# A retention layer feeding two dense networks: decay masks by scans, two blocks of tokens sharing the accumulator banks of the first expert, and state products issued with the value products

## The chip, the core and the metric

The kernel runs on one core of a Trainium2 chip. The core has a matrix engine (TensorE, rows "PE", its weight loads "PEld"), three elementwise engines (VectorE "DVE", ScalarE "ACT", GpSimd "POOL") and a queue engine (SyncE "SP") that issues the transfers; 16 DMA engines carry these out. The metric is the time of one execution on the device, in microseconds (us), as the median of several runs.

## What is computed

Three stages follow each other: a block-wise retention (linear attention with a decay `lam` per head), a mixture of four experts with given gates, and one dense network.

```python
def _attn_ref(q, k, v, lam):            # B, H, S, D = 2, 8, 768, 64
    rel = pos[:, None] - pos[None, :]   # pos: places in a block
    Dmask = np.where(rel >= 0, lam[:, None, None] ** rel[None], 0.0)
    for b in range(nb):
        intra = einsum('bhic,bhjc->bhij', qb, kb) * Dmask[None]
        intra = einsum('bhij,bhjd->bhid', intra, vb)
        inter = einsum('bhid,bhde->bhie', qb * lam_pow[None], kv_state)
        out[:, :, sl] = intra + inter
        kv_state = lam_block * kv_state + einsum('bhsd,bhse->bhde', kb * rev_pow, vb)
...
def _moe_ref(x, domain_probs, w1, w2):  # 1536 tokens, width 512, 4 experts of 1024
    p = domain_probs / (domain_probs.sum(-1, keepdims=True) + 1e-09)
    for e in range(E):
        out += p[:, e:e + 1] * (np.maximum(x @ w1[e], 0.0) @ w2[e])
...
def _moe2_ref(x, w_in, w_out):          # inner width 2048
    h = x @ w_in
    return (h * (1.0 / (1.0 + np.exp(-h)))) @ w_out
```

## The kernel before

**Retention.** It works on blocks of 128 tokens, six per batch (c = 0 to 5), so twelve units u = 2c + b. A unit is cut into pieces. `prep` makes `qs` (queries times `qdec`, the powers of `lam`) and `old` (the decayed state), both on GpSimd. `scores` makes `ks` (decayed keys, GpSimd), multiplies keys by queries into two banks `s` on TensorE, and VectorE multiplies these by the mask `dmask` into `a`. `mix` forms the output `xps` from the state and from `a` and the values. `carry` forms the state products `sps` from `ks` and the values. These matmuls take plain float32.

**Masks.** `powers` writes the powers of `lam` into a small tile `z` by seven doublings on VectorE, stores it to device memory (`zd`) and loads it back with overlapping addresses: `dmask` then holds, for key place j and query place i, the power for i and j, and `qdec` the powers for a query place. Before and after the first scores, `keep_warm` gives TensorE matmuls on zeros ("warm").

**Experts.** Every operand of a matmul is kept as a high and a low part (`xhi`, `xlo`; weights `ua`, `ub` for up and `dh`, `dl` for down; hidden `hhi`, `hlo`), and three products are summed. ScalarE makes the high part, VectorE or GpSimd the low one (`split`, line 142). Phase "a" does the first 512 tokens (blocks c = 0 and 1 of both batches, 256 columns each), one expert after the other in eight steps f; a step has a `gemm1` (12 matmuls into `ph`) and, two steps later, a `gemm2` (12 matmuls into the four banks `po`). Weights come in pairs of steps: `("a", i)` serves f = 2i and 2i + 1, 512 KB up (`u`) and 512 KB down (`d`). For expert 0 the eight steps run once over columns 0 to 255 and once over columns 256 to 511, since block c = 1 is not ready earlier; each half has its own set of `po` banks, emptied by `evacuate`. Experts 1 to 3 run over 512 columns. In between come the pieces of units 2 to 11, spread over half-steps by `plan` and `attend`. Phase "a" has so 40 steps. The rest ("c" for the other 1024 tokens, "b" and "d" for the dense network) is the same in both kernels.

**Order.** All engines run their instructions in the order of the code, as `manual_schedule` says; transfers are issued by SP in that order as well, and a transfer into a buffer in use waits there for its readers, with all behind it.

## Time and profile before

| | |
|---|---|
| time, median of 3 runs | 816.2 us (815.89 to 816.4) |
| span of the profiled execution, first to last instruction | 814.1 us |
| TensorE busy | 807.5 us (99%) |
| VectorE, GpSimd, ScalarE busy | 529.7, 453.4, 326.4 us |
| first `gemm1` starts / step 16 (expert 1) starts | 15.67 / 77.30 us into the span |

Only the span is given of the profiled execution; its own time on the device is not listed. The span is 2.1 us under the median, for what lies around it. "Busy" of TensorE counts the warm matmuls and the switch from one kind of matmul to another, so 99% busy does not say that nothing can be taken out.

### The profile page before, as it was taken

What the parts mean: (1) busy time and instruction counts of PE and PEld (TensorE: products, weight loads), DVE (VectorE), ACT (ScalarE), POOL (GpSimd) and SP (SyncE); (2) the same over time, 40 slices, a digit from 0 to 9 for tenths busy, and PEclk for the clock granted to TensorE, in tenths of its full rate; (3) what the DMA queues carried; (4) which work ended last, traced back from release to release, by engine and by line L of the source; (5) the groups of instructions that cost most, each with busy time, mean ns of one, the idle gap of its engine ahead of it and who ended that gap; (6) DMA issues with size and microseconds to landing.
All of it is one profiled execution on the core that took longest, in us unless ns stands there. A gap on an engine that the chain in (4) does not pass through costs nothing.

```text
span 814.1 us, 11017 instructions
## 1 busy us (share of the span) xinstructions
PE 807.5 (99%) x4224; PEld 666.9 (82%) x4224; DVE 529.7 (65%) x762; ACT 326.4 (40%) x528; POOL 453.4 (56%) x333
## 2 busy tenths in 40 slices
PE   9999999999999999999999999999999999999998
PEld 5899877778888888888888888888888888888886
DVE  6375797545668588878888878865454345666666
ACT  3433332433446333333333333334454465444431
POOL 1824755525666666666666666754346666555631
PEclk9999999999999999999999999999999999999999
DMA  8885767533324223223322211122233131111002
GB/s 296 317 321 195 250 240 240 189 102 117 104 104 142 90 91 115 94 83 98 112 94 85 94 61 70 46 90 90 78 103 105 52 103 52 52 52 52 27 1 103
DMA packets 31434, 95.93 MB, mean 118 GB/s; under 512 B 3409, under 2 KB 5001, under 8 KB 31381
## 3 DMA queue, kind: packets, MB, share of 16 engines
q1 hardware_dynamic: 31380, 95.23, 35.1%
q8 instruction: 33, 0.54, 0.3%
q14 instruction: 21, 0.16, 0.1%
HBM read 83.65 MB, written 11.57 MB: 117 GB/s over the span
## 4 chain that ended last, share of the span: by engine, by line
PE 93%; DVE 3%; DMA 2%; issue 1%; ACT 1%; POOL 0%; SPq 0%; ACTq 0%; POOLq 0%
PE po L707 32%; PE po L525 14%; PE ph L470 14%; PE y L647 12%; PE x L647 8%; PE z L647 8%; PE warm L299 1%; PE s L374 1%; PE xps L401 1%; DMA words<-wts 1%; DMA u<-wts 1%; DVE dec L213 1%; DVE dec L209 1%; DVE tail L206 1%; PE xps L397 1%
## 5 line engine op out<-in xcount | busy, mean ns | idle before, releaser
L707 PE MATMUL po<-hlo,dh 128*128 128x512 f32 x384 | 149.6, 390 | 0.0
L707 PE MATMUL po<-hhi,dh 128*128 128x512 f32 x384 | 149.6, 390 | 0.0
L707 PE MATMUL po<-hhi,dl 128*128 128x512 f32 x384 | 149.6, 389 | 0.0
L719 DVE TENSOR_TENSOR acc<-po,acc 128x512 f32<-128x512 f32 x176 | 117.2, 683 | 43.2 <-PE po L707 43.2
L142 POOL TENSOR_TENSOR ub<-u,ua 128x256 fp32r<-128x256 f32 (+2 forms) x48 | 74.8, 1559 | 107.4 <-ACT ua L141 103.1
L142 POOL TENSOR_TENSOR dl<-d,dh 128x1024 fp32r<-128x1024 f32 (+1 forms) x48 | 114.3, 2380 | 28.8 <-ACT dh L141 28.8
L664 POOL TENSOR_TENSOR s<-s,s 128x512 f32<-128x512 f32 x48 | 63.2, 1319 | 50.3 <-ACT s L659 50.2
L142 POOL TENSOR_TENSOR uc<-u,uc 128x512 fp32r<-128x512 f32 x24 | 31.2, 1301 | 96.7 <-ACT uc L141 96.7
L707 PEld LDWEIGHTS po<-hhi,dl 128*128 128x128 f32 x384 | 72.1, 188 | 15.0
L707 PEld LDWEIGHTS po<-hhi,dh 128*128 128x128 f32 x384 | 72.1, 188 | 14.9
L707 PEld LDWEIGHTS po<-hlo,dh 128*128 128x128 f32 x384 | 72.1, 188 | 14.9
L497 ACT ACTIVATE hhi<-ph 128x512 fp32r<-128x512 f32 x40 | 23.9, 599 | 97.0 <-DVE ph L491 83.3
L142 POOL TENSOR_TENSOR ub<-us,ua 128x1024 fp32r<-128x1024 f32 x24 | 58.4, 2433 | 5.3 <-ACT ua L141 5.3
L525 PE MATMUL po<-hhi,dh 128*128 128x512 f32 (+1 forms) x224 | 58.7, 364 | 0.0
L525 PE MATMUL po<-hhi,dl 128*128 128x512 f32 (+1 forms) x224 | 57.7, 360 | 0.0
L525 PE MATMUL po<-hlo,dh 128*128 128x512 f32 (+1 forms) x224 | 57.6, 359 | 0.0
L470 PE MATMUL ph<-xhi,ua 128*128 128x512 f32 (+1 forms) x224 | 55.6, 371 | 1.2 <-DVE hlo L481 0.7
L141 ACT ACTIVATE dh<-d 128x1024 fp32r<-128x1024 f32 (+1 forms) x52 | 51.3, 988 | 9.2 <-POOL ub L142 2.6
L470 PE MATMUL ph<-xhi,ub 128*128 128x512 f32 (+1 forms) x224 | 53.1, 359 | 0.0
L470 PE MATMUL ph<-xlo,ua 128*128 128x512 f32 (+1 forms) x224 | 53.1, 359 | 0.0
L498 DVE TENSOR_TENSOR hlo<-ph,hhi 128x512 fp32r<-128x512 f32 x40 | 27.7, 692 | 27.8 <-ACT hhi L497 27.8
L470 PEld LDWEIGHTS ph<-xhi,ua 128*128 128x128 f32 x224 | 37.9, 189 | 9.4 <-DVE hlo L481 0.9
(128 smaller groups left out, 1577.7 us busy)
## 6 DMA issues: line engine op xcount, KB each, us to landing
u<-wts SPq DMA_DIRECT2D x32, 512.0 KB, 3.6
d<-wts SPq DMA_DIRECT2D x32, 512.0 KB, 3.7
words<-wts SPq DMA_DIRECT2D x32, 512.0 KB, 5.1
wd<-dec SPq DMA_DIRECT2D x32, 256.0 KB, 3.1
u<-wd SPq DMA_DIRECT2D x16, 512.0 KB, 3.7
d<-wd SPq DMA_DIRECT2D x16, 512.0 KB, 3.7
qkt<-qk SPq DMA_DIRECT2D x12, 512.0 KB, 5.9
kvt<-kv SPq DMA_DIRECT2D x10, 512.0 KB, 5.6
```

Source lines behind the costliest of these rows:

```text
L141: nc.scalar.activation(out=hi, in_=src, func=AF.Copy)
L142: eng.tensor_tensor(out=lo, in0=src, in1=hi.bitcast(F32), op=ALU.subtract)
L206: nc.vector.tensor_scalar(out=tail, in0=low, scalar1=2.0 ** -29, scalar2=None, op0=ALU.mult)
L209: nc.vector.scalar_tensor_tensor(out=f, in0=high, scalar=3, in1=f, op0=ALU.logical_shift_left, op1=ALU.bitwise_or,)
L470: nc.tensor.matmul(pt[:, :n], lhsT=w, rhs=x[:, k, o:o + n], start=(j == 0), stop=(j == len(ops) - 1),)
L497: nc.scalar.activation(out=hi, in_=pt, func=AF.Copy)
L498: nc.vector.tensor_tensor(out=lo, in0=pt, in1=hi.bitcast(F32), op=ALU.subtract)
L525: nc.tensor.matmul(po_t[d][:, :n], lhsT=w[:, d * P:(d + 1) * P], rhs=h[:, :n], start=(begin and j == 0), stop=(last and j == 2),)
L647: nc.tensor.matmul(to, lhsT=a[:, k * P:(k + 1) * P], rhs=b[:, k], start=(first and j == 0), stop=(j == len(ops) - 1), skip_group_check=not ...
L664: nc.gpsimd.tensor_tensor(out=t, in0=a, in1=b, op=ALU.add)
L707: nc.tensor.matmul(po, lhsT=w, rhs=h, start=(j == 0), stop=(j == len(ops) - 1))
L719: nc.vector.tensor_tensor(out=a, in0=po, in1=a, op=ALU.add)
```

## The change

**Masks.** `lam` is loaded as one row, spread over the 128 partitions by a matmul with a row of ones (`spread`), and VectorE makes `dmask` by eight scans (`lam_scan`: each element is the one before it times `lam`, plus an element of `unit`, which is 1 where key and query place meet). `qdec` comes from four more scans, after the first `gemm1`. The store and the two loads of `dmask` and the two of `qdec` are gone. The matmuls on zeros are cut from eight to two shorter ones. The sums and products for the gates move to GpSimd.

**Expert 0.** Steps 0 to 3 run f = 0 to 3 on columns 0 to 255, steps 4 to 7 run f = 4 to 7 on all 512 columns, steps 8 to 11 run f = 0 to 3 on columns 256 to 511. All add into one set of four `po` banks, emptied once. Phase "a" has 36 steps. The first four steps, their splits and units 2 and 3 are written out in a fixed order.

**State products.** For c > 0 they are issued inside `mix`, behind the value products and into the free half of the same bank.

The core of the diff:

```diff
+    lam_t = acst.tile([P, H + NPAIR], F32, name="lamt")
+
+    def lam_scan(out, col, add, initial):
+
+        nc.vector.tensor_tensor_scan(
+            out=out,
+            data0=lam_t[:, col:col + 1].to_broadcast([P, P]),
+            data1=add,
+            initial=initial,
+            op0=ALU.mult,
+            op1=ALU.add,
+        )
+
...
     def powers():
-        z = acst.tile([H, 2 * P], F32, name="z")
-        nc.sync.dma_start(out=z[:, P:P + 1], in_=lam)
-        nc.vector.memset(z[:, :P - 1], 0.0)
-        nc.vector.memset(z[:, P - 1:P], 1.0)
+        row = acst.tile([1, H + P], F32, name="row")
+        nc.sync.dma_start(
+            out=row[:, :H], in_=bass.AP(lam.tensor, lam.offset, [[0, 1], [1, H]])
+        )
+        nc.gpsimd.memset(row[:, H:], 1.0)
+        nc.gpsimd.memset(zeros, 0.0)
+        unit_t = acst.tile([P, P], F32, name="unit")
+        nc.gpsimd.affine_select(
+            out=unit_t,
+            in_=zeros[:, 0],
+            pattern=[[1, P]],
+            base=1 - P,
+            channel_multiplier=1,
+            compare_op=ALU.not_equal,
+            fill=1.0,
+        )
+        load_qk(0, 0)
         load_probs()
-        for b in range(B):
-            load_qk(0, b)
-        m = 1
-        while m < P:
-            o = P - 1 + m
-            nc.vector.tensor_scalar_mul(z[:, o + 1:o + 1 + m], z[:, P:o + 1], z[:, o:o + 1])
-            m *= 2
-        nc.sync.dma_start(out=zd, in_=z)
-        gates()
-        for b in range(B):
-            load_kv(0, b, [1])
-        for m in range(2):
-            nc.sync.dma_start(
-                out=dmask[:, 2 * m:2 * m + 2],
-                in_=bass.AP(
-                    zd.tensor, zd.offset + m * H * P, [[1, P], [2 * P, NPAIR], [1, P]]
-                ),
-            )
+        load_kv(0, 0, [1])
+        load_qk(0, 1)
+        load_kv(0, 1, [1])
         load(0)
         for b in range(B):
             load_kv(0, b, [0])
+        load(0)
+        load(1)
+
+        spread = psum.tile([P, H], F32, tag="po0", name="spread")
+        nc.tensor.matmul(spread, lhsT=row[:, H:], rhs=row[:, :H], start=True, stop=True)
+        keep_warm(NPAIR)
+        nc.vector.tensor_copy(lam_t[:, :H], spread)
+        for h in range(H):
+            lam_scan(dmask[:, h // 2, h % 2], h, unit_t, 0.0)
+
+    def query_powers():
         for t in range(2):
-            nc.sync.dma_start(
-                out=qdec[t * D:(t + 1) * D],
-                in_=bass.AP(
-                    zd.tensor, zd.offset + t * 2 * P + P, [[0, D], [4 * P, NPAIR], [1, P]]
-                ),
-            )
-        nc.gpsimd.memset(zeros, 0.0)
-        keep_warm(3)
+            nc.vector.tensor_copy(lam_t[t * D:(t + 1) * D, H:], lam_t[t * D:(t + 1) * D, t:H:2])
+        for p in range(NPAIR):
+            lam_scan(qdec[:, p], H + p, zeros[:, 0], 1.0)
 
     def keep_warm(n):
         warm = psum.tile([P, NPAIR, P], F32, tag="po3", name="warm")
-        for _ in range(n):
...
         def mix():
 
 
-            xps = [bank([P, 2, P], "xps", t if u == 0 else None) for t in range(2)]
+            both = [bank([P, NPAIR, P], "xps", t if u == 0 else None) for t in range(2)]
+            xps = [t[:, :2] for t in both]
+            sps = both[1][:, 2:].rearrange("p a (n d) -> p (a n) d", d=D)
...
+            if c > 0:
+                products(sps)
...
-        def carry():
+            if c > 0:
+                renew(sps)
+
+        def products(sps):
             if c + 1 == NC:
                 return
-            sps = bank([P, NPAIR, D], "sps")
             for p in range(NPAIR):
                 for t in range(2):
                     nc.tensor.matmul(
@@ -430,6 +453,10 @@
                         start=True,
                         stop=True,
                     )
+
+        def renew(sps):
+            if c + 1 == NC:
+                return
             if c == 0:
                 nc.vector.tensor_copy(state[b], sps)
             else:
@@ -438,17 +465,25 @@
                 nc.gpsimd.tensor_tensor(out=state[b], in0=box["old"], in1=new, op=ALU.add)
             load_kv(c + 1, b)
-        return [prep, scores, mix, carry]
+        def carry():
+            sps = bank([P, NPAIR, D], "sps")
+            products(sps)
+            renew(sps)
+
+        return [prep, scores, mix, carry, keys]
...
     groups = {
-        "a": [(0, 0, CW), (0, CW, CW)] + [(g, 0, TW) for g in range(1, E)],
+        "a": [(0, 0, CW), (0, 0, TW), (0, CW, CW)] + [(g, 0, TW) for g in range(1, E)],
         "b": [(0, 0, TW)],
     }
     steps = {
-        "a": [(gi, f) for gi in range(E + 1) for f in range(NF)],
+        "a": [(0, f) for f in range(NN)]
+        + [(1, f) for f in range(NN, NF)]
+        + [(2, f) for f in range(NN)]
+        + [(gi, f) for gi in range(3, E + 2) for f in range(NF)],
         "b": [(0, f) for f in range(2 * NF)],
     }
...
-        end = {"b": len(steps["b"]) - 1}.get(ph, NF - 1 if g == 0 else len(steps["a"]) - 1)
-        begin = f == 0 and (ph == "b" or g < 2)
-        last = i == end or (ph == "a" and g == 0 and f == NF - 1)
+        n_steps = len(steps[ph])
+        starts, ends = ((0, 2 * NN + NF - NN), (NN + NF - 1, n_steps - 1)) if ph == "a" else (
+            (0,), (n_steps - 1,)
+        )
+        begin, last = i in starts, i in ends
         whi, wlo = (t[:, fw % 2] for t in down_t[ph, fw // 2])
...
             nc.tensor.matmul(
-                po_t[d][:, :n],
+                po_t[d][:, o:o + n],
                 lhsT=w[:, d * P:(d + 1) * P],
                 rhs=h[:, :n],
                 start=(begin and j == 0),
                 stop=(last and j == 2),
+                skip_group_check=(ph == "a" and g == 0),
             )
         if last:
-            evacuate(ph, gi, ds)
...
-        piece(0, 0)
-        piece(1, 0)
-        piece(0, 1)
-        piece(1, 1)
-        keep_warm(5)
+        na = len(steps["a"])
+        PREP, SCORE, MIX, CARRY, KEYS = range(5)
+
+        piece(0, PREP)
+        piece(1, PREP)
+        piece(0, SCORE)
+        gates()
+        keep_warm(2)
+        piece(1, SCORE)
+        for u in range(B):
+            piece(u, KEYS)
+        piece(0, MIX)
         half_up(("a", 0), 0, nc.vector)
-        piece(0, 2)
-        piece(1, 2)
+        piece(1, MIX)
+        half_up(("a", 0), 1, nc.vector, False)
         for b in range(B):
             load_qk(1, b)
-        half_up(("a", 0), 1, nc.vector)
+
+        gemm1("a", 0)
+        query_powers()
+        half_up(("a", 1), 0, nc.vector)
+        half_up(("a", 1), 1, nc.gpsimd, False)
+
+        gemm1("a", 1)
+        for u in range(B):
+            piece(u, CARRY)
+        load(1)
+        load(0, 2)
+        piece(2, PREP)
         half_down(("a", 0), 0, nc.vector)
-        half_down(("a", 0), 1, nc.vector)
-        gemm1("a", 0)
-        split_half(("a", 1), 0, nc.vector)
-        piece(0, 3)
-        piece(1, 3)
-
-        def span(u0, u1):
-            order = []
-            for u in range(u0, u1):
-                order += [(u, 1)] + [(u + 1, 0)] * (u + 1 < B * NC) + [(u, 2), (u, 3)]
-            return [(lambda u=u, j=j: piece(u, j)) for u, j in order]
-
-        plan = {0: span(2, 4), 1: span(4, 6), 2: span(6, 9), 3: span(9, 12)}
+        half_down(("a", 0), 1, nc.gpsimd)
+
+        gemm1("a", 2)
+        piece(2, SCORE)
+        piece(3, PREP)
+        gemm2("a", 0)
+        store_gates()
+
+        gemm1("a", 3)
+        piece(2, MIX)
+        half_down(("a", 1), 0, nc.vector)
+        gemm2("a", 1)
+        piece(3, SCORE)
+        half_down(("a", 1), 1, nc.vector)
+        piece(4, PREP)
+        w_tiles(wp, ("a", 2))
+        for n in range(2):
+            half_up(("a", 2), n, nc.gpsimd)
+
+        gemm2("a", 2)
+        piece(3, MIX)
+        gemm2("a", 3)
+
+        slots = 2 * 3 * NF
+        todo = {}
+        for u in range(2 * B, NC * B):
+            at = (u - 2 * B) * slots // (NC * B - 2 * B)
+            todo.setdefault(at + 1, []).append((u, SCORE))
+            if u + 1 < NC * B:
+                todo.setdefault(at + 2, []).append((u + 1, PREP))
+            todo.setdefault(at + 4, []).append((u, MIX))
 
...
-        todo, mixing = [], []
-        na = len(steps["a"])
-        for i in range(na):
+            for u, j in todo.get(slot - 2 * NN, ()):
+                piece(u, j)
+
+        mixing = []
+        for i in range(NN, na):
             gi, f = steps["a"][i]
-            if f == 0:
...
+            if f == 0 and gi == 3:
+                first.close()
...
+            gemm1("a", i)
+            attend(2 * i)
             flush()
-            if 2 <= i < na - 1:
+            if NN + 2 <= i < na - 1:
                 gemm2("a", i - 2)
-            attend(2 * f + 1)
```

In the listings below a row is a line of the kernel, an operation, output and inputs, the output's shape and how many follow each other. VectorE, from its first instruction, before (`z`: the powers; `gate`: the gates' sums; `a`: masked scores):

```order
L262 MEMSET z 8x127
L263 MEMSET z 8x1
...
L270 TENSOR_SCALAR z<-z 8x64
L314 TENSOR_TENSOR gate<-gate 12x128
...
L318 RECIPROCAL gate<-gate 12x128
L320 TENSOR_TENSOR gate<-gate 12x128 x4
L382 TENSOR_TENSOR a<-s,dmask 128x256 x8
L142 TENSOR_TENSOR ub<-u_157,ua 128x2x256
```

and of the change (a scan is printed as SCALAR_TENSOR_TENSOR):

```order
L298 COPY lamt<-spread 128x8
L258 SCALAR_TENSOR_TENSOR dmask<-lamt,unit 128x128 x8
L399 TENSOR_TENSOR a<-s,dmask 128x256 x4
L332 RECIPROCAL gate<-gate 48x32
L399 TENSOR_TENSOR a<-s,dmask 128x256 x4
L437 TENSOR_TENSOR xlo<-xps,xhi 128x2x128 x2
L142 TENSOR_TENSOR ub<-u_142,ua 128x2x256
```

The eight scans now stand in front of the first masked scores on the engine that needs them, where before a transfer stood; the gates' sums have left the engine.

TensorE, from its first matmul to the first `gemm1`, before (`warm`: matmuls on zeros; `s`: scores of both units; `xps`: their outputs; `ph`: the hidden columns):

```order
L299 MATMUL warm<-zeros 128x512 x3
L374 MATMUL s<-qkt 128x128 x16
L299 MATMUL warm<-zeros 128x512 x5
L401 MATMUL xps<-a,kvt 64x128 x16
L470 MATMUL ph<-xhi,ua 128x256 x4
```

and of the change:

```order
L296 MATMUL spread<-row 128x8
L310 MATMUL warm<-zeros 128x512
L391 MATMUL s<-qkt 128x128 x8
L310 MATMUL warm<-zeros 128x256
L391 MATMUL s<-qkt 128x128 x8
L420 MATMUL xps<-a,kvt 64x128 x16
L505 MATMUL ph<-xhi,ua 128x256 x4
```

The matmuls on zeros shrink, and the scores of the two units are apart.

TensorE again, around the outputs of unit 3 in the narrow steps, before (`sps`: state products):

```order
L397 MATMUL xps<-qs,state_116 64x128 x8
L401 MATMUL xps<-a,kvt 64x128 x8
L525 MATMUL po<-hhi,dh 128x256 x4
L525 MATMUL po<-hhi,dl 128x256 x4
L525 MATMUL po<-hlo,dh 128x256 x4
L426 MATMUL sps<-kvt,ks 64x64 x8
L470 MATMUL ph<-xhi,ua 128x256 x4
```

and of the change:

```order
L416 MATMUL xps<-qs,state_115 64x128 x8
L420 MATMUL xps<-a,kvt 64x128 x8
L449 MATMUL xps<-kvt,ks 64x64 x8
L562 MATMUL po<-hhi,dh 128x256 x4
L562 MATMUL po<-hhi,dl 128x256 x4
L562 MATMUL po<-hlo,dh 128x256 x4
L505 MATMUL ph<-xhi,ua 128x512 x4
```

The state products no longer stand alone between two blocks of expert work, and the `gemm1` behind is already 512 columns wide.

## Rows read from the trace of the kernel before

**Rows 1.** The page's chain that ended last, shares of the span by engine.

```profile
PE 93%; DVE 3%; DMA 2%; issue 1%; ACT 1%; POOL 0%; SPq 0%; ACTq 0%; POOLq 0%
```

**Rows 2.** Waits of PE, whole span: who, releaser, total us, times, longest.

```profile
PE ph L470 <- DVE hlo L481: 0.7, 1, 0.7
...
PE sps L426 <- ACT xraw L412: 0.2, 1, 0.2
PE xps L397 <- DVE a L382: 0.2, 1, 0.2
```

**Rows 3.** Timeline, 0 to 16 us: start, us, instruction, count, [idle before].

```profile
1.31 5.49 PE L299 MATMUL warm<-zeros 128*128 128x512 f32 x6 [1.31 <-POOL zeros L293]
...
2.09 1.76 DVE L270 TENSOR_SCALAR z<-z 8x1 f32<-8x1 f32 x7 [1.10 <-DMA z<-lam]
...
6.73 2.07 PE L374 MATMUL s<-qkt 64*128 64x128 f32 x32
...
8.73 4.56 PE L299 MATMUL warm<-zeros 128*128 128x512 f32 x10
...
10.42 2.74 DVE L382 TENSOR_TENSOR a<-s,dmask 128x256 f32<-128x256 f32 x8 [3.61 <-DMA dmask<-zd]
...
12.63 0.63 ACT L141 ACTIVATE ua<-u 128x512 fp32r<-128x512 f32 x1 [10.62 <-DMA u<-wts]
...
13.22 1.97 PE L401 MATMUL xps<-a,kvt 128*64 128x128 f32 x32
...
15.23 0.66 ACT L415 ACTIVATE xhi<-xps 128x256 fp32r<-128x256 f32 x2 [0.21 <-PE xps L401]
...
15.67 0.78 PE L470 MATMUL ph<-xhi,ua 128*128 128x256 f32 x4 [0.48 <-ACT xhi L415]
```

**Rows 4.** Busy time by stretch; the last three: granted clock, DMA share, GB/s.

```profile
6.00:7.00 1.00, 1.00 (x5) 0.28 (x6) 0.81 (x4) 0.00 (x0) 0.00 (x0) 1.00 1.00 383
...
18.00:20.00 2.00, 2.00 (x31) 1.93 (x26) 1.60 (x4) 1.38 (x3) 0.00 (x0) 1.00 1.03 418
```

**Rows 5.** Groups of DVE by shape, 0 to 27 us: count, busy us, mean ns.

```profile
L142 DVE TENSOR_TENSOR ub<-u,ua 128x512 fp32r<-128x512 f32 x4 | 3.3, 828 | 0.2
...
L481 DVE SCALAR_TENSOR_TENSOR hlo<-ph,hhi 128x256 fp32r<-128x256 f32 x3 | 1.3, 417 | 3.1 <-ACT hhi L480 3.1
L318 DVE RECIPROCAL gate<-gate 12x128 f32<-12x128 f32 x1 | 0.9, 940 | 0.0
...
L314 DVE TENSOR_TENSOR gate<-gate 12x128 f32<-12x128 f32 x1 | 0.3, 271 | 0.0
```

**Rows 6.** Timeline of PE around one and around two blocks of state products.

```profile
17.33 1.15 PE L426 MATMUL sps<-kvt,ks 128*64 128x64 f32 x32
...
18.41 0.75 PE L470 MATMUL ph<-xhi,ua 128*128 128x256 f32 x4
...
33.63 0.64 PE L470 MATMUL ph<-xlo,ua 128*128 128x256 f32 x4
...
34.20 0.69 PE L426 MATMUL sps<-kvt,ks 128*64 128x64 f32 x16
...
34.81 0.75 PE L525 MATMUL po<-hhi,dh 128*128 128x256 f32 x4
...
35.40 0.64 PE L525 MATMUL po<-hhi,dl 128*128 128x256 f32 x4
```

**Rows 7.** The chain in order of time: start, us, what.

```profile
52.34 1.44 PE po L525 x12
...
184.70 2.72 PE ph L470 x12
```

**Rows 8.** Timeline, 20 to 24 us, GpSimd, VectorE and TensorE.

```profile
20.46 1.30 POOL L344 TENSOR_TENSOR qs<-qkt,qdec 128x512 f32<-128x512 f32 x1 [4.55 <-DMA qkt<-qk]
...
21.07 1.25 DVE L142 TENSOR_TENSOR ub<-u,ua 128x512 fp32r<-128x512 f32 x1
...
23.73 0.74 PE L470 MATMUL ph<-xhi,ua 128*128 128x256 f32 x4 [0.74 <-DVE hlo L481]
```

More of the change, by code (lines that the diff above doesn't have):

```diff
@@ L27 @@
 HW = DM // 2
-FIRST = 6
-PREP = 1
+DECODE = 4
+GI = 32
+NN = 4
 NW = E * NF // 2
@@ L354, in prep, with keys @@
                 box["old"] = old
-        def scores():
+        def keys():
             if c + 1 < NC:
@@ L368, in scores @@
                 box["ks"] = ks
+        def scores():
+            if c > 0:
+                keys()
             s = [bank([P, NPAIR, P], "s", t if u == 0 else None) for t in range(2)]
@@ L838 @@
-        plan = {0: span(2, 4), 1: span(4, 6), 2: span(6, 9), 3: span(9, 12)}
-        def attend(slot):
-            skip = FIRST if gi == 0 else 0
-            if gi == 0 and slot == PREP:
-                piece(2, 0)
-            n, m = len(todo), 2 * NF - skip
-            for j in range(max(slot - skip, 0) * n // m, max(slot + 1 - skip, 0) * n // m):
-                todo[j]()
-        todo, mixing = [], []
-        na = len(steps["a"])
-        for i in range(na):
-            gi, f = steps["a"][i]
-            if f == 0:
-                todo = plan.get(gi, [])
-                if gi == 2:
-                    first.close()
-                elif gi == E:
-                    flush()
-                    store_decoded()
-                    att.close()
-                    tmp["comb"] = pool(ctx, "comb")
-                    tmp["sums"] = pool(early, "sums", side="right")
-                    mixing = combine(*x_raw)
-            if i:
-                gemm1("a", i)
-            attend(2 * f)
+        gemm1("a", 0)
@@ new lines, in attend @@
+        def attend(slot):
+            for u, j in todo.get(slot - 2 * NN, ()):
+                piece(u, j)
+        mixing = []
+        for i in range(NN, na):
+            gi, f = steps["a"][i]
+            if f == 0 and gi == 3:
+                first.close()
+            elif f == 0 and gi == E + 1:
+                flush()
+                store_decoded()
+                att.close()
+                tmp["comb"] = pool(ctx, "comb")
+                tmp["sums"] = pool(early, "sums", side="right")
+                mixing = combine(*x_raw)
+            gemm1("a", i)
+            attend(2 * i)
@@ L891 @@
+            if i == NN:
+                for n in range(2):
+                    half_down(("a", 2), n, nc.gpsimd)
+                w_tiles(wp, ("a", 3))
+                half_up(("a", 3), 0, nc.gpsimd)
+            elif i == NN + 1:
+                half_up(("a", 3), 1, nc.gpsimd)
+                half_down(("a", 3), 0, nc.gpsimd)
+            elif i == NN + 2:
+                half_down(("a", 3), 1, nc.gpsimd)
+            elif i >= 9 and i % 2:
                 if i < na - 3:
-                    split_up(("a", (i - 5) // 2))
+                    split_up(("a", (i - 1) // 2))
```

78 lines of the change are left out of this document (33 added, 45 removed).

## The prediction, written before the result

> **What bounds the kernel now.** The first view to read is the chain of work that ended last: 93% of it is TensorE [rows 1]. The second is what TensorE waits for: behind the first `gemm1` it waits three times, 0.7, 0.2 and 0.2 us [rows 2]. From there to the end it has the next matmul ready nearly always. So time can come out in three ways only: an earlier first `gemm1`, less work on TensorE behind it, or those 1.1 us. The timeline shows the first way: until 15.67 TensorE does little that the output needs [rows 3]. The scores run from 6.73 and would let VectorE go on at once, but it sits 3.61 us until the mask has come back from device memory, at 10.42; then come 2.74 of masked scores, 1.97 of value products and 0.66 of copies. Meanwhile TensorE multiplies zeros for 4.56 us. The other ways are in the timeline of the experts, below.
>
> **The start.** It is a race of three chains.
>
> *Mask.* `lam` is in the core at 2.09, when VectorE's first power starts [rows 3]. The spread (8 columns) and its copy I put at 0.7 together, between next to nothing and the 0.92 of a 512-column warm matmul (5.49 over 6) plus the 0.42 of a 256-element VectorE row [rows 3, 5]. GpSimd's `unit` tile (128x128) is a quarter of the 1.30 us row of `qs` [rows 8], 0.33, begun at about 1.4; it hides behind `lam` unless it takes over 1.4 us. Scans start at 2.8. The trace has no scan. It is not quicker than a plain two-input operation of that length, 0.27, as each element needs the one before; from above I bound it by the costliest row of that length, the reciprocal, 0.94 [rows 5]. I take 0.42, that of a two-operator instruction on twice the elements, since multiply and add follow each other. Eight are 3.4 us (2.2 to 7.5): done at 6.2.
>
> [...]
>
> *Scores.* Both units' queries and keys were there at 6.73. Unit 0's now go first and are half of it, 0.52 MB, which is 1.4 us at 383 GB/s [rows 4]: there at 5.3. How fast TensorE is then depends on its clock. [...] In the change the work begins at 2.1, pauses from about 4 to 5.3 and goes on. No row says when the clock rises then; the ends are that it is high from 5.3 on, or low until the first `gemm1`, and I take the middle of this stretch (5.3 to some 13), 9.2. [...] So unit 0's end at 7.4, the 256-column warm at 8.3, unit 1's at 9.8. VectorE masks at 0.34 a piece (2.74 over 8) and ends at 10.5; `xps` of unit 0 takes TensorE to 10.8, of unit 1 to 11.8. ScalarE then has in order `xhi` of unit 0 (0.66, to 11.5), half of `ua` (0.63, to 12.1) and the first half of unit 1's `xhi`: first `gemm1` at 12.5.
>
> *Weights.* 1.05 MB were in the core at 6.73. The first `u` now follows with the values, again 1.05 MB, 2.6 us at some 400 GB/s [rows 4], and with no transfer ahead that waits for a store: it lands near 9.3 instead of 12.63 [rows 3], ahead of its turn on ScalarE.
>
> The start so gains 15.7 - 12.5 = **3.2**. [...]
>
> **Fewer, wider matmuls.** Twelve matmuls of 256 columns take 1.44, of 512 columns 2.72 [rows 7]: two narrow blocks cost 0.16 more than one wide. Four f by two (`gemm1`, `gemm2`) are eight such pairs of blocks: **-1.3**. One set of banks instead of two changes nothing on TensorE; VectorE empties it in four instructions instead of eight.
>
> **State products joined.** Standing alone, 16 of them cost TensorE this: four `ph` matmuls from 33.63 (0.48, a third of 1.44) would end at 34.11; the four of the next block begin at 34.81 and take until 35.40 instead of 0.48. That is 35.40 - 0.48 - 34.11 = 0.81. Where 32 follow each other, start to next block is 1.08 against 0.61 for 16 [rows 6], so 16 more cost 0.47. The other 0.34 is the change from one kind of matmul to the other and back, which the join spares. Units 2 to 9: 8 x 0.34 = **-2.7**; none of it is the other end. What hides the edit's own price is that `ks` is put into GpSimd's queue with the scores, ahead of the next unit's `qs`; if it came late, TensorE would stand in `mix` with a `gemm2` queued behind.
>
> **Waits.** The three of 1.1 us go or change places. A new one stands ahead of the third `gemm1`: it needs the low part `ub` of pair 1 from VectorE, and ahead of that stand `hlo` of the first step and the four `qdec` scans, 1.7 us. At the same time GpSimd has the other half of `ub`, then `qs`. These two engines take turns: VectorE's `ub` at 21.07 took 1.25, ending 0.55 after GpSimd's `qs` (20.46 + 1.30), while the other three of its four took 0.68 [rows 5, 8]. With `hlo` done at 14.9, copies 0.2, scans, one turn of 1.3 and `ub` 0.68 I come to 18.8; TensorE, with the second `gemm1` (to 15.4), the two carries (1.28) and four matmuls of the third, is there at 17.2. That is 1.6, with a second turn 2.9, without any 0.3. I take 2.2 in all, net **+1.1**. Loads are covered: behind the carries (16.7) four transfers stand up to `u` of pair 2, 0.52 MB each at 418 GB/s [rows 4], so by 22, and the first wide step comes after 30.
>
> **Sum.** -3.2 - 1.3 - 2.7 + 1.1 = -6.1. The profiled span of 814.1 becomes 808.0, and with the 2.1 us by which the median lies above it, **810.1**.
>
> **Rivals.**
>
> *The clock stays low* through the first steps, since less work on zeros is left. For it: in the row the clock rose only behind work without a pause, and here there is one. Against: from 5.3 on work is nearly unbroken. Unit 1's scores would end at 10.4, `xps` at 14.4, `gemm1` start at 14.8 and its first block last 1.4 longer: the start is lost by 0.5, and the sum is +0.5 - 1.3 - 2.7 + 1.1 = -2.4: 813.8. [...] Chance 0.13.
>
> *Slow scans*, 0.94 each: gain at the start 1.0, and four `qdec` scans 2.1 longer in the wait: -1.0 - 1.3 - 2.7 + 3.2 = -1.8: 814.4. For it: a chain from element to element. Against: only the reciprocal is that slow. Chance 0.10.
>
> *The join spares nothing*, because 64-wide products behind 128-wide ones switch as well, or `ks` is late: 812.8. Chance 0.12.
>
> *Slower:* each scan waits for a turn of GpSimd. All read two tiles in the core's memory, as the `ub` of rows 8 does. Twelve turns of 1.3 would be 15.6, less 1.2 of slack (scans 6.2, scores 7.4) and the one turn counted: +13 against -6.1, 823. It decides from five turns on. Against: between 2 and 8 us GpSimd has only small sums for the gates. Chance 0.06.
>
> *Weights late:* a transfer that I see covered is not, and the first wide step waits for what the start gained: 815 to 816. Chance 0.05.
>
> **Chances and range.** The forecast has 0.54. About 0.2%, 1.6 us, is what a measurement of this kernel tells from no change. Forecast, low clock, no join and most of the slow scans are faster by more: 0.88. No difference 0.05, slower 0.07. Below, full clock and a wait of 0.3 give -4.6 - 1.3 - 2.7 - 0.8 = -9.4, so 806.8; above, the range goes to the low clock: 807.0 to 813.8.
>
> **What would show it.** [...] The prediction is wrong if the first `gemm1` comes at 15 or later, if TensorE waits over 4 us in the written-out steps, or if TensorE's time from there to expert 1 does not shrink.

## The result, and the profile after

The changed kernel takes 808.8 us (median of 4 runs, 808.49 to 809.77), the kernel before 816.13 beside it on the same chip; the ratio is 0.9912, 95% interval 0.9898 to 0.9926. The profiled execution has a span of 808.0. The results also list each execution's own time: in all of them it is 1.8 us above the span. So the profiled execution of the change took 809.77, the longest of its four, and that of before, by the same difference, 815.9, near the shortest of its runs.

The page's chain that ended last, shares of the span by engine, where [rows 1] had 93% for PE:

```profile
PE 97%; DMA 1%; DVE 0%; POOL 0%; issue 0%; ACT 0%; SPq 0%; ACTq 0%
```

What PE waits for in the changed kernel (engine, tile and line <- releaser: us in total, times, longest), against [rows 2]:

```profile
PE s L391 <- DMA qkt<-qk: 1.1, 1, 1.1
PE ph L505 <- DVE ub L142: 1.0, 1, 1.0
PE ph L505 <- ACT xhi L436: 0.5, 1, 0.5
PE xps L420 <- PE xps L420: 0.2, 1, 0.2
PE ph L505 <- POOL ub L142: 0.2, 1, 0.2
```

The 0.7 for `hlo` and the two waits of 0.2 of before are gone. Behind the first `gemm1` 1.0 for `ub` at the third `gemm1` and 0.2 for another `ub` have come; ahead of it stand the waits for queries and keys and for `xhi`.

The timeline of the changed kernel to the first `gemm1` (start, us, engine, line, instruction, count, [idle before]):

```profile
2.54 2.08 PE L310 MATMUL warm<-zeros 128*128 128x512 f32 x2
...
2.92 2.64 DVE L258 TENSOR_TENSOR_SCAN dmask<-lamt,unit 128x128 f32<-128x128 f32 x8
...
4.67 2.08 PE L391 MATMUL s<-qkt 64*128 64x128 f32 x16
...
6.68 1.22 PE L310 MATMUL warm<-zeros 128*128 128x256 f32 x2
6.78 1.42 DVE L399 TENSOR_TENSOR a<-s,dmask 128x256 f32<-128x256 f32 x4 [1.22 <-PE s L391]
...
8.99 1.16 PE L391 MATMUL s<-qkt 64*128 64x128 f32 x16 [1.09 <-DMA qkt<-qk]
...
10.18 1.42 DVE L399 TENSOR_TENSOR a<-s,dmask 128x256 f32<-128x256 f32 x4 [1.73 <-PE s L391]
...
13.28 0.79 PE L505 MATMUL ph<-xhi,ua 128*128 128x256 f32 x4 [0.47 <-ACT xhi L436]
```

A scan takes 2.64 / 8 = 0.33, and all masks are done at 5.57, before unit 0's scores are (6.75). Sixteen score matmuls take 2.08 for unit 0 and 1.16 for unit 1: TensorE's two speeds, as in [rows 3]. The trace's own record of the granted clock rises at 8.07. Between the two units TensorE waits 1.09 for unit 1's queries and keys. In both units the first masked score `a` begins only when the last of the sixteen matmuls has ended, at 6.78 and 10.18. The chain in order of time (start, us, what) says what set the start:

```profile
2.47 6.47 DMA qkt<-qk
```

The load issued at 2.47 landed 6.47 later. In that time the DMA engines moved little. Busy time by stretch, the last three columns granted clock, DMA share and GB/s, against 383 for 6 to 7 us in [rows 4]:

```profile
5.00:6.00 1.00, 1.00 (x12) 1.00 (x12) 0.57 (x2) 0.00 (x0) 0.77 (x3) 1.00 0.81 147
6.00:7.00 1.00, 1.00 (x9) 0.78 (x8) 0.22 (x1) 0.00 (x0) 0.28 (x1) 1.00 0.68 270
```

The granted clock reads 1.00 here because the trace has no record of it before the first rise, at 8.07; the 2.08 for sixteen score matmuls shows the lower of the two speeds.

The timeline around the third `gemm1`:

```profile
16.18 2.42 DVE L258 TENSOR_TENSOR_SCAN qdec<-lamt,zeros 128x128 f32<-128x128 f32 x4
...
16.56 1.44 POOL L142 TENSOR_TENSOR ub<-u,ua 128x512 fp32r<-128x512 f32 x1 [2.40 <-ACT ua L141]
...
18.52 0.66 DVE L142 TENSOR_TENSOR ub<-u,ua 128x512 fp32r<-128x512 f32 x1
...
19.24 0.73 PE L505 MATMUL ph<-xhi,ub 128*128 128x256 f32 x4 [1.02 <-DVE ub L142]
```

Four `qdec` scans take 2.42 here against 1.32 for four of the mask: beside GpSimd's `ub` they lose a turn, 1.1. VectorE's `ub` stands behind them.

The state products inside `mix` of unit 2:

```profile
25.13 1.09 PE L420 MATMUL xps<-a,kvt 128*64 128x128 f32 x16
26.05 0.64 PE L449 MATMUL xps<-kvt,ks 128*64 128x64 f32 x16
26.62 0.74 PE L562 MATMUL po<-hhi,dh 128*128 128x256 f32 x4
```

From the value products' start to the next block it is 26.62 - 25.13 = 1.49.

In sum: the first `gemm1` came at 13.28 instead of 15.67, 2.39 earlier. From there to the last matmul's start it is 790.63 instead of 794.29, 3.67 less (before: 15.67 to 809.96; after: 13.28 to 803.90). Together 6.06.

### The profile page after: what moved, and what is told of

Read it like the earlier page. It is cut to its first block, busy times and chain, and to the rows that moved or that the text cites. A ratio compares the mean times of both kernels' runs of the same rounds, so it can differ in the third digit from the quotient of the medians.

```text
span 808.0 us, 10790 instructions
## 1 busy us (share of the span) xinstructions
PE 799.2 (99%) x4118; PEld 660.0 (82%) x4118; DVE 514.2 (64%) x750; ACT 325.6 (40%) x524; POOL 467.9 (58%) x345
## 4 chain that ended last, share of the span: by engine, by line
PE 97%; DMA 1%; DVE 0%; POOL 0%; issue 0%; ACT 0%; SPq 0%; ACTq 0%
PE po L744 32%; PE po L562 17%; PE ph L505 16%; PE y L684 12%; PE x L684 8%; PE z L684 8%; PE xps L420 2%; PE s L391 1%; DMA qkt<-qk 1%; PE xps L416 1%; PE xps L449 0%; POOL dl L142 0%; DVE qdec L258 0%; POOL ub L142 0%; ACT hhi L515 0%
## 5 line engine op out<-in xcount | busy, mean ns | idle before, releaser
L142 POOL TENSOR_TENSOR ub<-u,ua 128x256 fp32r<-128x256 f32 (+2 forms) x49 | 77.2, 1576 | 115.8 <-ACT ua L141 103.6
L142 POOL TENSOR_TENSOR dl<-d,dh 128x1024 fp32r<-128x1024 f32 (+1 forms) x49 | 116.9, 2387 | 30.4 <-ACT dh L141 30.4
L701 POOL TENSOR_TENSOR s<-s,s 128x512 f32<-128x512 f32 x48 | 69.3, 1446 | 44.5 <-ACT s L696 44.4
L562 PE MATMUL po<-hhi,dl 128*128 128x512 f32 (+1 forms) x208 | 55.8, 373 | 0.0
L562 PE MATMUL po<-hlo,dh 128*128 128x512 f32 (+1 forms) x208 | 55.8, 373 | 0.0
L505 PE MATMUL ph<-xhi,ua 128*128 128x512 f32 (+1 forms) x208 | 53.4, 378 | 0.5 <-ACT xhi L436 0.5
L505 PEld LDWEIGHTS ph<-xhi,ub 128*128 128x128 f32 x208 | 37.3, 188 | 9.2 <-DVE ub L142 1.2
```

What stands on the lines that cost most here:

```text
L142: eng.tensor_tensor(out=lo, in0=src, in1=hi.bitcast(F32), op=ALU.subtract)
L505: nc.tensor.matmul(pt[:, :n], lhsT=w, rhs=x[:, k, o:o + n], start=(j == 0), stop=(j == len(ops) - 1),)
L562: nc.tensor.matmul(po_t[d][:, o:o + n], lhsT=w[:, d * P:(d + 1) * P], rhs=h[:, :n], start=(begin and j == 0), stop=(last and j == 2), skip ...
L701: nc.gpsimd.tensor_tensor(out=t, in0=a, in1=b, op=ALU.add)
```

## The experiments

One table for all. "Ratio" is to the kernel before on the same chip; "start" is the first `gemm1` of the profiled execution, "rest" from there to the start of the last matmul, "clock" the first rise in the trace's record of the granted clock.

| kernel | median us | ratio, 95% | start | rest | clock |
|---|---|---|---|---|---|
| before | 816.13 | 1 | 15.67 | 794.29 | 6.80 |
| changed | 808.8 | 0.9912, 0.9898 to 0.9926 | 13.28 | 790.63 | 8.07 |
| e1_qk_first | 807.97 | 0.9902, 0.9887 to 0.9917 | 11.45 | 790.66 | 5.90 |
| e2_ub_first | 809.6 | 0.9924, 0.991 to 0.9939 | 12.55 | 790.76 | 8.86 |
| e3_both | 808.27 | 0.991, 0.9893 to 0.9927 | 13.46 | 790.71 | 10.96 |
| e4_no_join | 820.17 | 1.005, 1.0033 to 1.0066 | 13.86 | 800.65 | 12.17 |
| e4b_no_join | 812.44 | 0.9958, 0.9943 to 0.9972 | 12.27 | 793.55 | 6.03 |
| e5_halves | 810.84 | 0.9935, 0.9919 to 0.9952 | 13.81 | 791.60 | 12.54 |
| e6_old_masks | 813.42 | 0.9971, 0.9961 to 0.9982 | 17.63 | 789.48 | 9.93 |
| e7_no_warm | 810.53 | 0.9936, 0.9921 to 0.9951 | 15.34 | 790.37 | 15.51 |
| e7b_more_warm | 810.82 | 0.9936, 0.9923 to 0.995 | 15.37 | 790.34 | 9.03 |
| e8_before_join | 813.53 | 0.997, 0.9958 to 0.9981 | 15.14 | 792.72 | 5.14 |
| e9_early_qdec | 806.93 | 0.9888, 0.9874 to 0.9901 | 11.73 | 789.01 | 5.81 |
| e10_early_warm | 808.25 | 0.9907, 0.9893 to 0.992 | 13.15 | 789.20 | 9.41 |

Where the code behind the first `gemm1` is as good as the same (changed, e1, e2, e3, e7, e7b) the rest agrees within 0.42 us, while the start lies anywhere from 11.45 to 15.37. e1 and e3 even have the same code up to the first `gemm1`, and 2.0 us lie between their two profiled starts; the changed kernel, e2, e4, e4b and e5 have the same order up to there too, and lie between 12.27 and 13.86. So the rest is a sharp measure from one profile, and the start is not: for it the medians count more.

### e1_qk_first: unit 1's queries and keys loaded second

```diff
         load_qk(0, 0)
+        load_qk(0, 1)
         load_probs()
         load_kv(0, 0, [1])
-        load_qk(0, 1)
```

> Only the order of the first loads is changed: the queries and keys of unit 1 are issued right behind those of unit 0, ahead of the gates' probabilities and unit 0's values. Theory: the first gemm1 (13.28 in the changed kernel) hangs on this transfer, which lands at 8.94; landing near 7.5 it brings the scores of unit 1 to about 7.9, the first gemm1 to 12.1 and the span from 808.0 to about 806.8. [...]

The wait for `qkt` is gone, and the timeline has the scores of unit 1 at:

```profile
6.90 1.16 PE L391 MATMUL s<-qkt 64*128 64x128 f32 x16
```

The start is 11.45 in this profile, 1.83 sooner than in the changed kernel: more than the transfer's 1.1. The clock rose at 5.90 here, and the matmuls on zeros ahead of these scores take 0.70 instead of 1.22. By the medians 0.8 us is won, with intervals that overlap. What sets this start is the next transfer of the queue; the chain in order of time:

```profile
3.42 7.04 DMA u<-wts
```

The first `u` lands at 10.46, where the prediction had 9.3.

### e2_ub_first and e3_both: `ub` ahead of the `qdec` scans, alone and with e1

```diff
         gemm1("a", 0)
-        query_powers()
         half_up(("a", 1), 0, nc.vector)
+        query_powers()
```

> On VectorE the first half of the low part ub of pair 1 goes ahead of the four qdec scans. Theory: the wait of 1.0 us ahead of the second four matmuls of the third gemm1 goes, nothing takes its place, and the span falls by 1.0 to 807.0. Rival: qs and old of unit 2 come later by 0.7 to 1.4 on GpSimd with dl behind them, and the wait comes back at the mix of unit 2 or at the second gemm2; span 807.6 to 808.2.

> Both edits of the order together. Theory: the gains add, since one is ahead of the first gemm1 and one behind it: span near 805.8, time 2.2 us under the changed kernel's. Rival: an earlier start only makes the third gemm1 wait longer, for GpSimd or for a load that has not landed; then little more than the better one of the two, 806.8 to 807.4.

The waits of PE in e2_ub_first, and its timeline around the scans:

```profile
PE s L391 <- DVE state L461: 1.0, 1, 1.0
```

```profile
16.02 1.29 POOL L142 TENSOR_TENSOR ub<-u,ua 128x512 fp32r<-128x512 f32 x1 [1.89 <-ACT ua L141]
16.07 1.44 DVE L304 COPY lamt<-lamt 64x4 f32<-64x4 f32 x2
...
17.55 1.37 DVE L258 TENSOR_TENSOR_SCAN qdec<-lamt,zeros 128x128 f32<-128x128 f32 x4
```

The wait for `ub` is gone, and one of the same size stands behind the third `gemm1`: the copies of the state are queued behind the scans on VectorE, and the next scores, which need the banks that these copies empty, wait for them. The rest is 790.76 against 790.63. The rival was right that the wait comes back, and wrong on where: it had `qs` and `old` late on GpSimd and the wait at `mix` or the second `gemm2`. The turn is not gone either. It fell on the two copies of `lamt` ahead of the scans, 1.44 beside GpSimd's `ub` where they take 0.33 in the changed kernel, and the scans take 1.37. What costs is the time of copies and scans on VectorE in this place, a turn included, whatever stands first. e3 shows the same wait of 1.0. Its profiled start fell late, with the clock at 10.96 and a wait of 0.46 for unit 0's queries and keys, and its time (ratio 0.991 against 0.9912) does not differ from the changed kernel's: the gains did not add.

### e4_no_join and e4b_no_join: the state products alone again

In both `mix` no longer issues `products` and `renew`; `carry` does so again for every c, in a place of its own. In e4 it stands behind the next unit's `ks`, in e4b ahead of the next unit's scores (the diff is e4b's):

```diff
-            if c > 0:
-                products(sps)
...
-        gemm2("a", 1)
+        gemm2("a", 1, [0, 1])
+        piece(2, CARRY)
+        gemm2("a", 1, [2, 3])
...
+        piece(3, CARRY)
...
+            todo.setdefault(at + 5, []).append((u, CARRY))
```

> The state products of units 2 to 9 stand alone again, half a step or more behind the mix, in a bank of their own. Theory: each costs 0.34 for the change of kind of matmul to and fro, eight of them 2.7: span 810.7. Rival: the join saved nothing and the wide steps or the waits made the gain: span 808.0 to 808.4.

> The state products of units 2 to 9 stand alone again, but each ahead of the next unit's scores, so that GpSimd's single ks buffer comes free in time (in e4_no_join it did not, and GpSimd stood 9 us). From the first gemm1 to the last matmul the changed kernel takes 790.6. Theory: eight times 0.34 more, 793.3, with waits of TensorE as in the changed kernel; time about 811.5. Rival: the gain of the join is in GpSimd's queue and in earlier loads, not in TensorE's change of kind; then new waits for GpSimd stand in the written-out steps and make up most of the difference, whatever its size.

e4 measured my misplacing, not the join. `ks` has one buffer; with `carry` behind the next unit's `ks`, GpSimd cannot write it until the late products, from 34.6 here, have read the old one. GpSimd's row, and the busy time of the stretch in which TensorE then stood 4.0 for `ub`:

```profile
35.40 1.06 POOL L374 TENSOR_TENSOR ks<-kvt,dmask 128x512 f32<-128x512 f32 x1 [9.16 <-issue]
```

```profile
44.00:53.00 9.00, 5.00 (x28) 3.44 (x26) 0.69 (x1) 2.61 (x5) 8.15 (x8) 0.82 0.94 295
```

GpSimd stood 9.16 and everything behind in its queue came late; by the chain of waits the load of the next values, too, was issued only at 38.95 and landed at 44.72, and `ub` behind the next `ks` ended at 49.58. The granted clock fell as well (0.82 over the stretch). A `carry` of its own has to stand ahead of the next unit's `ks`.

e4b is the clean test: the rest is 793.55, 2.92 more than in the changed kernel, 0.36 for each of the eight blocks against 0.34 in the prediction. TensorE's waits behind the first `gemm1` came out alike (0.8 for `ub`, 0.2 for `xraw` and the pause of 0.2 below, against 1.0 and 0.2 for `ub`), so the rival that the join's gain lies in GpSimd's queue falls. TensorE around `mix` and the products of unit 2:

```profile
24.18 1.09 PE L419 MATMUL xps<-a,kvt 128*64 128x128 f32 x16
25.21 0.50 PE L558 MATMUL po<-hhi,dh 128*128 128x256 f32 x2
...
25.78 0.40 PE L558 MATMUL po<-hlo,dh 128*128 128x256 f32 x2
26.31 0.69 PE L443 MATMUL sps<-kvt,ks 128*64 128x64 f32 x16
...
27.27 0.40 PE L558 MATMUL po<-hhi,dl 128*128 128x256 f32 x2
```

From the value products to the next block it is 1.03 here and 1.49 with the join: the products cost 0.46 there. Standing alone they cost, from the end of the block ahead (25.78 + 0.24) to the third matmul behind (27.27) less the 0.24 of two matmuls, 1.01, of which 0.2 is a pause ahead of them whose cause the trace does not name (26.02 to 26.31, where [rows 6] has 34.11 to 34.20): 0.81, the value of [rows 6].

### e5_halves: the four wide steps of expert 0 as two halves of 256 columns

```diff
+        parts = [(0, n)]
+        if ph == "a" and gi == 1:
+            parts = [(0, CW), (CW, TW)]
+        for a, z in parts:
...
-                po_t[d][:, o:o + n],
-                lhsT=w[:, d * P:(d + 1) * P],
-                rhs=h[:, :n],
+                    po_t[d][:, o + a:o + z],
+                    lhsT=w[:, d * P:(d + 1) * P],
+                    rhs=h[:, a:z],
```

> The four wide steps of expert 0 issue each block of matmuls as two of 256 columns, as before the change; the banks and the order stay. Theory: eight blocks cost 0.16 more each, 1.3 in all: 791.9 from the first gemm1 to the last matmul (790.6 in the changed kernel). Rival: these steps are paced by GpSimd and the loads (a wait for ub of 0.2 stands in one of them), and a longer block only fills waits: 790.6 to 791.0.

The rest grows by 0.98: 0.12 for each of eight blocks, where the prediction had 0.16. The timeline of two wide blocks in the changed kernel, one behind a switch of matmul kind and one not, each with the start of what follows:

```profile
38.52 1.19 PE L505 MATMUL ph<-xhi,ua 128*128 128x512 f32 x4
...
41.38 1.07 PE L505 MATMUL ph<-xhi,ua 128*128 128x512 f32 x4
...
58.13 1.09 PE L562 MATMUL po<-hhi,dh 128*128 128x512 f32 x4
...
60.88 0.64 PE L505 MATMUL ph<-xhi,ua 128*128 128x256 f32 x4
```

and, from e5_halves, a narrow block behind a switch and then the same two blocks as halves:

```profile
33.59 0.74 PE L570 MATMUL po<-hhi,dh 128*128 128x256 f32 x4
...
35.13 0.64 PE L509 MATMUL ph<-xhi,ua 128*128 128x256 f32 x4
...
39.19 0.74 PE L509 MATMUL ph<-xhi,ua 128*128 128x256 f32 x4
...
42.17 0.64 PE L509 MATMUL ph<-xhi,ua 128*128 128x256 f32 x4
...
59.43 0.64 PE L570 MATMUL po<-hhi,dh 128*128 128x256 f32 x4
...
62.30 0.64 PE L509 MATMUL ph<-xhi,ua 128*128 128x256 f32 x4
```

From start to start the wide blocks take 2.86 and 2.75, their halves 2.98 and 2.87: 0.12 more in either place. The narrow block behind a switch takes 35.13 - 33.59 = 1.54 against 1.44 [rows 7], so a switch costs both kinds about 0.1. The rival, at most 791.0, is ruled out, though these steps do pause for `ub`: TensorE waits 0.5 in e5's third wide `gemm1` against 0.2, while the fourth, which pauses in the changed kernel, does not in e5 (2.88 against 3.04). The pauses about cancel.

### e6_old_masks: the powers, the store and the loads of before, in the order of the change

The scans, `unit` and `spread` are taken out; the seven doublings, the store to `zd` and the loads of `dmask` and `qdec` stand where the change's loads allow it.

```diff
+        while m < P:
+            o = P - 1 + m
+            nc.vector.tensor_scalar_mul(z[:, o + 1:o + 1 + m], z[:, P:o + 1], z[:, o:o + 1])
+            m *= 2
+        nc.sync.dma_start(out=zd, in_=z)
...
-        for h in range(H):
-            lam_scan(dmask[:, h // 2, h % 2], h, unit_t, 0.0)
```

> The mask and the query powers come by way of device memory again, as before the change; all else is the changed kernel. Theory: the first masked scores wait until about 10.4 and the first gemm1 comes at about 15.2 instead of 13.3, but VectorE has no scans ahead of the third gemm1, so its wait of 1.0 goes: 789.6 from the first gemm1 to the last matmul, span 808.9. Rival: the scans are worth the whole 2.4 of the earlier start: first gemm1 at 15.7, span 810.4. Second rival: the mask was not what held the start and the shorter queue of loads was: first gemm1 at 13.5 or earlier.

The timeline, and the busy time of a stretch:

```profile
11.99 1.64 DVE L386 TENSOR_TENSOR a<-s,dmask 128x256 f32<-128x256 f32 x4 [8.14 <-DMA dmask<-zd]
...
13.39 3.76 PE L407 MATMUL xps<-a,kvt 128*64 128x128 f32 x32 [3.30 <-issue]
```

```profile
14.00:16.00 2.00, 2.00 (x23) 2.00 (x22) 1.14 (x4) 0.26 (x1) 1.10 (x5) 0.50 1.02 341
```

The start is 4.35 later than in the changed kernel: later than either theory, and later than before the change. The mask comes at 11.99, later than the 10.42 of before [rows 3], and why was not settled; with so few matmuls on zeros TensorE stands idle for 3.3 meanwhile, the granted clock, high from 9.93, falls to 0.50, and the value products take 3.76 instead of the 1.97 of [rows 3]. Scans and fewer warm matmuls belong together: with the mask early the two short calls on zeros are enough, with the mask late they are not. How much of the 4.35 is the mask's and how much the clock's was not taken apart. The rest is 789.48, 1.15 less than in the changed kernel, as its theory had it: without `qdec` scans VectorE has `ub` ready.

### e7_no_warm and e7b_more_warm: no matmuls on zeros, and twice 1024 columns

e7 leaves both out; e7b issues two of 512 columns at each of the two places instead of one of 512 and one of 256 (the diff is e7b's).

```diff
         keep_warm(NPAIR)
+        keep_warm(NPAIR)
...
-        keep_warm(2)
+        keep_warm(NPAIR)
+        keep_warm(NPAIR)
```

> Both matmuls on zeros are left out. [...] Theory: without them the rise comes at 10 or later, the first gemm1 at 13.5 to 15, time 0.5 to 2 us over the changed kernel's. Rival: the loads set the start, and TensorE's work from 4.6 on is enough: first gemm1 at 12.5 to 13.3, time within 0.5 of the changed kernel's.

> The changed kernel with two matmuls on zeros of 512 columns at each of the two places instead of one of 512 and one of 256. Theory: unit 1's queries and keys set the start (landed at 8.94 in the changed kernel), and the extra matmuls end before both units' loads, so the first gemm1 stays at 13.3 or comes up to 0.4 sooner by a clock that is high when unit 1's scores begin: time 808.4 to 808.8. Rival A: the rise of the clock sets the start: with more work it is at 7 or sooner, the first gemm1 at 12 to 12.5, time 807.5 to 808. Rival B: the matmuls on zeros push the scores out: up to 0.9 later, 809.7.

Timeline of TensorE in e7_no_warm:

```profile
9.16 2.08 PE L390 MATMUL s<-qkt 64*128 64x128 f32 x16 [2.50 <-DMA qkt<-qk]
...
11.17 3.68 PE L419 MATMUL xps<-a,kvt 128*64 128x128 f32 x32
```

and in e7b_more_warm:

```profile
2.56 4.21 PE L311 MATMUL warm<-zeros 128*128 128x512 f32 x4
...
6.69 2.08 PE L392 MATMUL s<-qkt 64*128 64x128 f32 x16
8.70 2.45 PE L311 MATMUL warm<-zeros 128*128 128x512 f32 x4
...
11.09 1.16 PE L392 MATMUL s<-qkt 64*128 64x128 f32 x16
```

Without them the granted clock rises only at 15.51, the rise of which the theory speaks, and both scores (2.08 for sixteen) and the value products (3.68 for 32) run at the lower speed: the start is 15.34, the time 2.0 us above the changed kernel's by the ratios, at the upper end of the theory. With more of them it is as late, 15.37: they stood in the way. I had priced a call as one row of 512 columns, but each call is two matmuls in the trace (x4 for two calls), so 2.1 at the low clock and not 0.9; the scores of unit 0 begin at 6.69 instead of 4.67. The rival that they push the scores out was right, with more than it said. Both directions lose about the same, for opposite reasons.

### e8_before_join: the kernel before with the join alone

```diff
+            both = [bank([P, NPAIR, P], "xps", t if u == 0 else None) for t in range(2)]
+            sps = both[1][:, 2:].rearrange("p a (n d) -> p (a n) d", d=D)
...
+            if c > 0:
+                products(sps)
```

> The kernel before with one part of the change alone: the state products of units with c > 0 are issued inside mix, behind the value products, into the free half of the same bank. Masks, order and narrow steps stay as before. Theory: eight blocks lose their own switch between kinds of matmul, 0.34 us each, so first gemm1 to last matmul falls from 794.3 to about 791.6, with the first gemm1 where it was (15.7), and the time is 2.7 below before, about 813.4. Here units 4 to 9 and 2, 3 are all joined as in the change. Rival A: the gain seen in the changed kernel needs the wide steps around the products; then 793.5 or more. Rival B: the decay of the state and the state's renewal come at another time, a wait takes the gain back: then a row of waits for a state or a ks of over 1 us.

The rest fell by 1.57 (the expected 2.7 less a new wait). The time, 813.53, meets the expected 813.4 by luck: this profile's start is also 0.53 earlier than that of before, with the same order up to there. PE's waits:

```profile
PE xps L399 <- DVE a L382: 1.3, 2, 1.2
```

That was 0.2 before [rows 2]; with the sums of waits behind the first `gemm1` at 2.0 against 1.1, the matmuls themselves gave 1.57 + 0.9 = 2.5. The second rival, a wait that takes back part, was right, though it is not for a state or `ks`: the masked scores `a` stand on VectorE behind an `hlo` that was late. The same edit is worth 2.9 in an order that was laid out for it and 1.6 in one that was not.

### e9_early_qdec and e10_early_warm: the two levers together

e9 is e1 with the `qdec` scans right behind the mask scans, where VectorE idles; e10 is e9 with a warm matmul of 512 columns ahead of `spread` and the one behind it cut to 256.

```diff
         for h in range(H):
             lam_scan(dmask[:, h // 2, h % 2], h, unit_t, 0.0)
+        query_powers()
...
         gemm1("a", 0)
-        query_powers()
```

> The changed kernel with unit 1's queries and keys loaded right behind unit 0's, and the four qdec scans moved right behind the mask scans on VectorE, ahead of the first masked scores. Theory: VectorE idles there until the scores are done, so the scans cost little (mask scans end 5.6, qdec 1.5 more, 7.1, scores of unit 0 end at 6.7: up to 0.4 late for the first masked scores), and the wait of 1.0 for ub at the third gemm1 goes without another taking its place: first gemm1 to last matmul 789.6 (790.63 in the changed kernel), first gemm1 at 11.5 to 12 if the clock rises by 8, so a time of about 806.7. Rival A: the scans ahead of the masked scores delay the start by their full 1.3, so that nothing is gained against the kernel with only the loads swapped (807.97). Rival B: the wait for ub stays, since GpSimd's other half and qs hold it, then 790.6.

> The kernel with early loads and early qdec scans, and one matmul on zeros of 512 columns more ahead of the spread (it begins as soon as the zeros are written, near 1.4), with the one behind the spread cut to 256 columns. Theory: the start varies with the moment at which the clock rises (5.9 to 12.5 us in profiles so far, first gemm1 at 11.45 to 13.86); with TensorE at work sooner it rises at 7 or before, the first gemm1 comes at 11.0 to 11.5 and the time is 0 to 1 us below that of the same kernel without the extra matmul. Rival: the moment of the rise does not follow these small matmuls; the first gemm1 then lies anywhere from 11.4 to 13.9, and the time is the same or later by what the extra matmul delays the spread (up to 0.6).

PE's waits in e9_early_qdec:

```profile
PE xps L421 <- DVE a L400: 0.3, 1, 0.3
PE ph L506 <- POOL ub L142: 0.2, 1, 0.2
```

The wait for `ub` is gone and no other took its place. The rest is 789.01, 1.65 under e1, for a start 0.28 later (the 0.3 for `a`, behind scans that end at 7.2). 806.93 us is the fastest of the study: by the ratios 1.1 us under e1 and 2.0 under the changed kernel; the intervals of the two barely overlap. e10's extra matmul did not do what I wanted of it:

```profile
3.45 0.59 PE L297 MATMUL spread<-row 1*128 1x8 f32 x2
```

`spread` came 1.4 later, every scan with it, and the clock rose only at 9.41, although TensorE had been at work nearly without a pause since 1.44: the rival. The time is about 1.5 above e9's by the ratios, where the rival had at most 0.6.

## Why the prediction came out as it did

The forecast was 810.1 with a span of 808.0; measured were 808.8 and 808.0. Its direction holds, and each of its four terms came by the mechanism that it named; three of them were off in size. The start gained 0.8 less and the wider matmuls 0.3 less, the waits cost 1.0 less. These cancel: that the span was met to 0.1 is luck.

**Start, -3.2: mis-sized in this execution, 2.39.** The mask chain was right in each link and a little quick (0.33 for a scan instead of 0.42, done at 5.57 instead of 6.2). Two steps failed behind it. Unit 1's queries and keys were taken as there when their turn came; they stood behind the gates' and unit 0's values in the queue and landed at 8.94, where the forecast had the scores begin at 8.3. e1 removes that wait, but it is not the same in every execution: with the same order of loads unit 1's scores begin at 7.75 in e2, which does not wait, and at 7.99, 8.32 and 8.26 in e4b, e4 and e5. The other step is in all these profiles: the forecast let VectorE end 0.7 behind unit 1's scores, at 10.5, so two of its four pieces beside them; all four `a` stand behind the scores and end at 11.60, 1.45 after them, which is 0.7 of the start. The scores' ends at 7.4 and 9.8 rest on 1.03 for sixteen matmuls behind the clock's rise, half of the 2.07 of [rows 3], and on twice that ahead of it, an estimate that no run had shown; the change showed 1.16 and 2.08. Against the lost time stood a clock that rose at 8.07 and not at 9.2. For that rise the forecast had a pause of TensorE from 4 to 5.3, and there was none: it priced the first call on zeros as one row of 0.92, and the call is two, 2.08. As the rest of this code hardly varies (table), the median's gain of 7.3 leaves about 3.7 for the start (7.3 - 3.67, an estimate): the profiled execution has a late one.

**Wider matmuls, -1.3: 0.98** (e5). The 2.72 of [rows 7] is of a wide block among wide ones; here they take 2.75 and 2.86.

**Join, -2.7: 2.9** (e4b), 2.5 without the order that suits it (e8).

**Waits, net +1.1: about 0.1.** The named wait came at the named place and for the named reason, but it is 1.0 instead of 1.6 and its companion 0.2, against 1.1 removed. The cheaper scans account for 4 x 0.09 = 0.36 of it. The turn fell on the scans and not on `ub` behind them. e2 shows that it cannot be put off within VectorE's queue, e9 that it can be taken out.

The three terms behind the first `gemm1` add up to 0.98 + 2.92 - 0.1 = 3.8, against 3.67 measured.

**Median over span: 1.8 instead of 2.1**, and the median itself lies 1.0 under the profiled execution. That is what makes 810.1 too high by 1.3. The gain of 4.6 in the lower end of the range is an estimate that no run shows: the earliest start, 11.45 in e1 with the clock up at 5.90, is a gain of 4.22.

**Rivals.** The clock did not stay low. The row that spoke for it, warm matmuls from 1.31 [rows 3] ahead of the rise at 6.80, is one case: in e10 nearly unbroken work from 1.44 saw the rise only at 9.41. It stayed low for longer where the matmuls on zeros are left out (e7), and fell again where the mask comes late (0.50 in e6, behind a pause of 3.3), with starts of 15.3 and 17.6, beyond the 14.8 that the rival worked out. Scans of 0.94 did not occur, so no run shows that rival's gain of 1.0 at the start; nor did the turns at the mask: eight scans ran at 0.33 beside GpSimd's small sums, and the one turn came at `qdec`. A scan's 0.33 for 128 elements is what a masked score takes for 256 (0.34, 2.74 over 8 [rows 3]), so the two-operator row that I took was the wrong neighbour. That the join spares nothing is ruled out by e4b. Late weights are not seen: none of TensorE's waits behind the first `gemm1` is for a load.

**Open.** Why the clock's first rise lies anywhere between 5.1 and 15.5 us, also for the same code (5.90 and 10.96 in e1 and e3), was not settled; nor why the DMA engines move so little near 5 us, nor why VectorE does not begin a unit's masks before all its scores are done.

## What to carry to other kernels

When a load is split so that one half can start sooner, follow the other half to its new place in the queue: its landing, not the engine's speed, may set the start (8.94 here, with TensorE waiting 1.09). An instruction moved onto an engine costs at the place where something waits behind it; the same scans cost 1.65 us behind the first `gemm1`, a turn of about 1.05 included, and a wait of 0.3 ahead of the masked scores. Matmuls on zeros are worth their time where TensorE would stand anyway, and each one too many stands ahead of the work: none and twice as many both lost 2.0 us. And compare blocks by one measure: from start to start, or end to end, not one against the other.

## What the runs showed of the hardware

- Four `qdec` scans took 2.42 in the changed kernel, 2.43 in e1 and 2.41 in e7, each beside a GpSimd `ub`, and 1.37 to 1.39 in e2, e3 and e9, where none ran beside them: one turn of about 1.05 for the group, not one for each scan. In e2 and e3 the two small copies of `lamt` (64x4) lost the turn instead, 1.44 and 1.43 against 0.33.
- The rate of the DMA engines fell to 147 GB/s between 5 and 6 us in the changed kernel, in e1 and in e9 alike, to 145 in e10 and 135 in e7; in e2 it was 142 between 4 and 5. The stretches beside had 175 to 394. The engines' busy share fell with it, to 0.41 to 0.54 (0.81 in the changed kernel), so it is not shown that they were slow. The kernel before has no such dip: 381 to 406 between 4 and 7.
- Behind a switch from plain float32 to the split products a block of twelve takes about 0.1 longer, wide (2.86 against 2.75) or narrow (1.54 against 1.44).
- A matmul of plain float32 on 512 columns is two in the trace, 2.08 for the first call at the lower clock.
- In every execution listed the time on the device is the span plus 1.8 us, so the spread between executions is in the span.
